# Loading 96 of 128 rows: two transfers of 48 rows in place of one of 128, from the fifth unit on

## The chip, the cores and the metric

The kernel runs on one core of one Trainium2 chip. The metric is device time in microseconds (us) of one execution, the median of several. A profiled execution gives a trace: each instruction with its engine, start and duration, what it waited for, and the packets that the 16 DMA engines moved. The engines are TensorE (PE, with its weight loads as PEld), VectorE (DVE), ScalarE (ACT), GpSimd (POOL) and SyncE (SP), which only issues transfers here.

## What is computed

A linear-attention layer whose state decays over time, and then a layer of eight experts of which each token uses one. Cut to what matters:

```python
def _attn_ref(r, k, v, w, u):                 # batch 4, heads 8, sequence 768, head size 48
    for t in range(S):
        cur = np.einsum('bhd,bhe->bhde', u[None] * kt, vt)
        y[:, :, t] = np.einsum('bhd,bhde->bhe', rt, state + cur)
        state = wt[:, :, :, None] * state + np.einsum('bhd,bhe->bhde', kt, vt)

def _moe_ref(x, ...):                         # 3072 tokens of 384 numbers, 8 experts, hidden size 1024
    e_idx = np.argmax(logits, axis=1)
    for e in range(E):
        h = np.maximum(x[mask] @ w1[e], 0.0)
        out[mask] = gate_w[mask, None] * (h @ w2[e])
```

## The kernel before

The attention part works through 24 units (`NU`), one for each batch element and stretch of 128 time steps. A unit holds all eight heads: heads come in pairs, and of the 128 partitions the first 48 rows belong to one head of each pair and rows 64 to 111 to the other. Rows 48 to 63 and 112 to 127 are padding: r and k are 0 and w is 1 there. The host lays r, k and w of a unit side by side in one array `rkw` of 128 rows by 1,541 numbers: r in columns 0 to 511, k in 512 to 1,023, w in 1,024 to 1,540.

Four buffers `ins[0..3]` (`NIN = 4`) of 128 partitions take turns: unit n is loaded into `ins[n % 4]`. `load(n, cuts)` of line 94 issues the transfers on SyncE's queue, one for each range of columns. Units 0 to 3 are loaded ahead of the loop. In the loop over i from -2 to 23, after the work of round i, SyncE issues in this order: v of unit i+3 (`loadv`, line 99), w of unit i+6, in some rounds a piece of a weight matrix (line 218, rounds 4 to 7 and from 18 on) or, later in the text, 128 rows of zeros to HBM (line 859, rounds 8 to 11), and r with k of unit i+6. A load into a buffer waits for those that read the buffer before: w for the scans of VectorE, r and k for GpSimd and ScalarE.

Round i (`att_iter`, line 287) works on three units at once. For unit a = i+2 VectorE runs a scan over w backward in time (line 295, giving B), takes four reciprocals, which it writes into w (297), and scans forward (298, giving E); GpSimd multiplies K from k and B (241) and G from r and k (306); ScalarE copies r into PSUM (235), and VectorE multiplies R (238). For unit m = i+1 TensorE transposes K (320) and multiplies K with R (345), VectorE masks the result (347), ScalarE copies v into zero-padded form (257), and TensorE adds to the state (359), which ScalarE scales (247). For unit z = i TensorE makes the output (372, 384, 387). VectorE or ScalarE with GpSimd forms the token rows (424, 421, 422), which TensorE transposes for the router (434, 440). In the rounds after the first ten units GpSimd also scatters the token rows to HBM, by expert (639). The order of the work is written out by hand; nothing is moved by a scheduler.

After some 120 us the expert blocks follow, bound by TensorE. Their first block reads rows that the scatters wrote. Later blocks read token rows in four loads of 32 partitions each (line 665).

Of the kernel before, what the change touches and what calls it, by code (L numbers as in the profile page):

```python
# [17 lines left out]
B, H, S, D = 4, 8, 768, 48  # L18
P = 128
# [39 lines left out]
def kernel(ctx: ExitStack, tc: tile.TileContext, rkw, vt, wf, cst, mid, wg, bias, w1, w2, out):  # L59
    nc = tc.nc  # L60
# [21 lines left out]
    NIN = 4  # L82
    ins = [pa.tile([P, 1600], F32, name=f"in{i}", bufs=1) for i in range(NIN)]
# [9 lines left out]

    def load(n, cuts=((0, 1541),)):
        for c0, c1 in cuts:
            nc.sync.dma_start(out=ins[n % NIN][:, c0:c1], in_=rkw[n, :, c0:c1])

    def loadv(n):
        nc.sync.dma_start(out=wt(n, "v", [P, VW], 4), in_=vt[n * P:(n + 1) * P, :])
# [4 lines left out]
    nc.vector.memset(wm, 0.0)  # L104
    cs = cp.tile([P, NCST], F32, name="cs")
    load(0, ((1024, 1541), (0, 1024)))
    load(1, ((1024, 1541),))
    nc.sync.dma_start(out=cs[:, 256:NCST], in_=cst[:, 256:NCST])
    loadv(0)
    load(1, ((0, 1024),))  # L110
    nc.gpsimd.memset(cs[:, 0:2 * P], 1.0)
    for c0, op in ((0, ALU.is_equal), (P, ALU.is_gt)):
# [1056 lines left out]
```

## Time and profile before

| what | value |
|---|---|
| median of 3 runs | 335.22 us (334.42 to 335.35) |
| the profiled execution | 336.19 us, of which the span of the trace 334.4 us |
| TensorE busy | 321.6 us, 96% of the span |
| TensorE weight loads | 293.1 us, 88% |
| VectorE busy | 214.4 us, 64% |
| ScalarE busy | 204.2 us, 61% |
| GpSimd busy | 196.6 us, 59% |
| moved by DMA | 58.66 MB, mean 175 GB/s |

TensorE's clock was granted at full speed almost throughout. Matmuls are pipelined and their ends are modelled, so a busy TensorE is not one at its peak. Shares over the whole span mix the attention rounds, where VectorE, GpSimd and ScalarE are nearly always busy, with the expert blocks, where they are not; a stage is to be read by itself. The chain that ended last, as the trace gives it, reaches back only 4 us from the end and says nothing of the attention rounds.

### The profile page before, as it was taken

To read this page: it belongs to the slowest core of one execution; us is meant where nothing else is said; L and a number is where in the kernel's file an instruction comes from. 1 tells how busy PE (TensorE), PEld (TensorE's weight loads), DVE (VectorE), ACT (ScalarE), POOL (GpSimd) and SP (SyncE) were. 2 spreads that over 40 slices of the span, in tenths; PEclk is the share of its full clock that TensorE was granted. 3 is DMA by queue.
4 is the path that set the end of the run, shared out by engine and by line. 5 is a ranking of instruction groups with operands and counts; after the bars stand their busy time and mean duration, and the time that the engine had idled before them with its cause. 6 is when DMAs were issued, how large, how long until landed. Compare 5 with 4: busy or idle time off the path is not lost. (4 is left out here: it accounts for less than half of the span.)

```text
span 334.4 us, 10126 instructions
## 1 busy us (share of the span) xinstructions
PE 321.6 (96%) x3942; PEld 293.1 (88%) x3943; DVE 214.4 (64%) x376; ACT 204.2 (61%) x467; POOL 196.6 (59%) x226
## 2 busy tenths in 40 slices
PE   6899998999999999999999999999999999999993
PEld 3689898988899988899889988998899889999993
DVE  6999997999999757795333965934560464054230
ACT  3887897787488775542521767656745855632150
POOL 7988987879999795676361680247024603450041
PEclk9999999999999999999999999999999999999998
DMA  7997888878998532426337037026544763360011
GB/s 273 406 347 245 294 280 241 285 243 240 301 309 263 163 97 97 95 95 215 143 119 213 0 84 250 0 73 169 185 167 165 214 233 97 95 212 5 0 74 32
DMA packets 35586, 58.66 MB, mean 175 GB/s; under 512 B 17297, under 2 KB 22089, under 8 KB 35528
## 3 DMA queue, kind: packets, MB, share of 16 engines
q1 hardware_dynamic: 32424, 48.45, 46.4%
q0 software_dynamic: 3104, 9.47, 7.6%
q8 instruction: 33, 0.54, 0.7%
q14 instruction: 25, 0.20, 0.2%
HBM read 57.86 MB, written 12.67 MB: 211 GB/s over the span
## 5 line engine op out<-in xcount | busy, mean ns | idle before, releaser
L224 POOL TENSOR_TENSOR wl<-raw,wh 128x768 fp32r<-128x768 f32 x20 | 39.0, 1954 | 73.8 <-ACT wh L223 73.7
L223 ACT CAST wh<-raw 128x768 fp32r<-128x768 f32 x48 | 39.3, 831 | 37.4 <-PE pU_d L731 23.3
L720 DVE SCALAR_TENSOR_TENSOR h<-pS_u,h 128x512 fp32r<-128x512 f32 (+2 forms) x39 | 23.2, 607 | 36.5 <-ACT h L718 36.3
L751 POOL DMA_INDIRECT out<-ot,xg x24 | 25.2, 1052 | 29.4 <-ACT ot L760 23.4
L224 DVE TENSOR_TENSOR wl<-raw,wh 128x768 fp32r<-128x768 f32 x28 | 31.0, 1113 | 14.8 <-ACT wh L223 14.4
L709 PE MATMUL pS_u<-xh,wh 128*128 128x512 f32 (+1 forms) x102 | 39.6, 388 | 0.0
L709 PE MATMUL pS_u<-xh,wl 128*128 128x512 f32 (+1 forms) x102 | 39.2, 385 | 0.0
L709 PE MATMUL pS_u<-xo,wh 128*128 128x512 f32 (+1 forms) x102 | 39.2, 384 | 0.0
L718 ACT ACTIVATE h<-pS_u 128x512 fp32r<-128x512 f32 (+1 forms) x34 | 19.8, 586 | 27.7 <-PE pS_u L709 25.4
L731 PE MATMUL pX_d<-wh,h 128*128 128x384 f32 x96 | 32.4, 337 | 0.0
L731 PE MATMUL pY_d<-wh,h 128*128 128x384 f32 x96 | 32.2, 335 | 0.0
L731 PE MATMUL pK_d<-wh,h 128*128 128x384 f32 x96 | 32.1, 334 | 0.0
L639 POOL DMA_INDIRECT xs<-xp,posT x24 | 26.1, 1088 | 9.3 <-issue 7.4
L306 POOL TENSOR_TENSOR G<-in 128x512 f32<-128x512 f32 x24 | 30.7, 1278 | 0.0
L241 POOL TENSOR_TENSOR K<-in,B 128x512 f32<-128x512 f32 x24 | 28.4, 1185 | 3.7 <-PE pY L387 1.7
L295 DVE TENSOR_TENSOR_SCAN B<-in,pX_d 128x516 f32<-128x516 f32 x24 | 29.3, 1219 | 1.8 <-DMA in<-rkw 1.8
L298 DVE TENSOR_TENSOR_SCAN E<-in,pX_d 128x516 f32<-128x516 f32 x24 | 29.5, 1229 | 0.8
L731 PE MATMUL pU_d<-wh,h 128*128 128x384 f32 x80 | 26.8, 334 | 0.0
L720 DVE SCALAR_TENSOR_TENSOR h<-pT_u,h 128x512 fp32r<-128x512 f32 (+2 forms) x17 | 9.6, 577 | 24.6 <-ACT h L718 24.6
L387 PE MATMUL pY<-v,A 128*64 128x48 f32 x368 | 25.3, 222 | 0.0
L347 DVE TENSOR_TENSOR A<-pS,m 128x768 f32<-128x768 f32 x24 | 22.8, 948 | 3.7 <-PE pS L345 3.6
L387 PEld LDWEIGHTS pY<-v,A 128*64 128x64 f32 x368 | 23.8, 138 | 0.0
(239 smaller groups left out, 860.8 us busy)
## 6 DMA issues: line engine op xcount, KB each, us to landing
raw<-w SPq DMA_DIRECT2D x24, 768.0 KB
in<-rkw SPq DMA_DIRECT2D x23, 512.0 KB
v<-vt SPq DMA_DIRECT2D x24, 288.0 KB
in<-rkw SPq DMA_DIRECT2D x23, 258.5 KB
wg<-wf SPq DMA_DIRECT2D x8, 576.0 KB
xl<-xs SPq DMA_DIRECT2D x20, 192.0 KB
raw<-w SPq DMA_DIRECT2D x16, 192.0 KB
xs<-zt SPq DMA_DIRECT2D x12, 193.0 KB
```

What stands on the lines that cost most here:

```text
L223: nc.scalar.copy(out=wh[k][:, sl], in_=raw[k][:, sl])
L224: (eng or (nc.vector, nc.gpsimd)[k]).tensor_tensor(out=wl[k][:, sl], in0=raw[k][:, sl], in1=wh[k][:, sl].bitcast(F32), op=ALU.subtract)
L241: nc.gpsimd.tensor_tensor(out=wt(a, "K", [P, 4, P]), in0=quarters(k), in1=quarters(T["B", a][:, 1:517])[:, :, 1:129], op=ALU.mult)
L295: nc.vector.tensor_tensor_scan(out=Bt[:, 516:0:-1], data0=w[:, 516:0:-1], data1=d1[:, 516:0:-1], initial=0.0, op0=ALU.mult, op1=ALU.max)
L298: nc.vector.tensor_tensor_scan(out=Et, data0=w[:, 0:516], data1=d1[:, 1:2].to_broadcast([P, 516]), initial=1.0, op0=ALU.mult, op1=ALU.max)
L306: nc.gpsimd.tensor_tensor(out=wt(a, "G", [P, 512]), in0=r, in1=k, op=ALU.mult)
L387: nc.tensor.matmul(out=yh[64:P, g, sw, hh], lhsT=A[:, hh, g, 1 + sw], rhs=vs[:, g, hh] if sw else v[:, h * D:(h + 1) * D], start=new and n ...
L639: rows_apart("xs", nc.gpsimd.indirect_dma_start(out=xs[:, :], out_offset=bass.IndirectOffsetOnAxis(ap=posT[:, n:n + 1], axis=0), in_=T["xp ...
L709: nc.tensor.matmul(out=pp, lhsT=wsrc[0][:, f, c * P:(c + 1) * P], rhs=xsrc[:, c], start=(n == 0), stop=(n == 3 * KC - 1))
L720: nc.vector.scalar_tensor_tensor(out=h2[:, o:o + c1 - c0], in0=pp[:, c0:c1], scalar=0.0, in1=hh[:, c0:c1].bitcast(F32), op0=ALU.max, op1=A ...
L731: nc.tensor.matmul(out=X["y", q][j], lhsT=hsrc[:, j * P:(j + 1) * P], rhs=wsrc[1][:, f], start=(f == 0 and n == 0), stop=(last and n == 2))
L751: ins = nc.gpsimd.indirect_dma_start(out=out[:, :], out_offset=bass.IndirectOffsetOnAxis(ap=xg[0:n, j, 1:2].bitcast(I32), axis=0), in_=ot[ ...
```

## The change

From the fifth unit on `load` issues, for each range of columns, two transfers in place of one: rows 0 to 47 and rows 64 to 111. The padding rows of a buffer are written by the first unit that it holds (units 0 to 3) and not again.

```diff
     def load(n, cuts=((0, 1541),)):
         for c0, c1 in cuts:
-            nc.sync.dma_start(out=ins[n % NIN][:, c0:c1], in_=rkw[n, :, c0:c1])
+            for q in (0, 64) if n >= NIN else (None,):
+                rows = slice(0, P) if q is None else slice(q, q + D)
+                nc.sync.dma_start(out=ins[n % NIN][rows, c0:c1], in_=rkw[n, rows, c0:c1])
```

`P` is 128 and `D` is 48. Each of units 4 to 23 is loaded with two ranges of columns, so its two transfers become four. All else is unchanged, the readers of the buffers included: they read all 128 rows.

## Rows read from the trace of the kernel before

**Rows 1.** Stretches of the span: us; busy time of PE, PEld, DVE, ACT, POOL; PEclk, DMA share, GB/s.

```profile
10.00:20.00 10.00, 8.70 (x208) 7.30 (x206) 9.86 (x13) 9.21 (x30) 9.70 (x18) 1.00 1.04 406
20.00:95.00 75.00, 72.00 (x1865) 66.28 (x1866) 70.87 (x102) 59.20 (x181) 65.50 (x72) 1.00 0.86 272
70.00:80.00 10.00, 9.50 (x251) 8.77 (x250) 9.83 (x15) 7.83 (x25) 8.88 (x9) 1.00 0.66 201
80.00:90.00 10.00, 8.98 (x235) 8.25 (x233) 9.67 (x14) 6.91 (x22) 9.60 (x10) 1.00 0.95 294
90.00:100.00 10.00, 9.99 (x263) 9.29 (x259) 9.62 (x14) 7.00 (x22) 9.44 (x10) 1.00 0.93 304
```

**Rows 2.** VectorE in order of time: start us, us, what, and idle time before it.

```profile
46.38 1.22 DVE L295 TENSOR_TENSOR_SCAN B<-in,pX_d 128x516 f32<-128x516 f32 x1
51.03 1.22 DVE L295 TENSOR_TENSOR_SCAN B<-in,pX_d 128x516 f32<-128x516 f32 x1
55.51 0.96 DVE L347 TENSOR_TENSOR A<-pS,m 128x768 f32<-128x768 f32 x1 [1.78 <-PE pS L345]
56.98 1.22 DVE L295 TENSOR_TENSOR_SCAN B<-in,pX_d 128x516 f32<-128x516 f32 x1
80.76 1.22 DVE L295 TENSOR_TENSOR_SCAN B<-in,pX_d 128x516 f32<-128x516 f32 x1
85.29 1.22 DVE L295 TENSOR_TENSOR_SCAN B<-in,pX_d 128x516 f32<-128x516 f32 x1
88.63 0.96 DVE L347 TENSOR_TENSOR A<-pS,m 128x768 f32<-128x768 f32 x1 [0.19 <-PE pS L345]
90.10 1.22 DVE L295 TENSOR_TENSOR_SCAN B<-in,pX_d 128x516 f32<-128x516 f32 x1
```

**Rows 3.** Waits of the compute engines: us in total, times, longest us.

```profile
DVE B L295 <- DMA in<-rkw: 1.8, 1, 1.8
POOL K L241 <- DMA in<-rkw: 1.2, 2, 0.7
```

**Rows 4.** Order of time, SyncE's issues and the readers of what they load.

```profile
44.77 0.33 SPq L96 DMA_DIRECT2D in<-rkw  x1
47.77 0.33 SPq L99 DMA_DIRECT2D v<-vt  x1
59.74 0.71 ACT L257 COPY vz<-v 64x192 f32<-64x192 f32 x2
61.20 1.22 DVE L295 TENSOR_TENSOR_SCAN B<-in,pX_d 128x516 f32<-128x516 f32 x1
```

**Rows 5.** TensorE in order of time, and the instruction queue from 20 to 95 us.

```profile
53.25 0.24 PE L384 MATMUL pY<-vz,A 128*64 128x96 f32 x1 [1.10 <-issue]
84.33 0.57 PE L272 MATMUL pT<-cs,G 128*64 128x2 f32 x13 [1.02 <-issue]
q8 instruction: 14, 0.23, 1.2%
```

**Rows 6.** Four loads of 32 rows: their issue, and the stretch (columns as rows 1).

```profile
134.46 1.97 SPq L665 DMA_DIRECT2D xl<-xs  x4
135.40:139.40 4.00, 4.00 (x32) 3.21 (x31) 3.67 (x9) 2.72 (x6) 2.85 (x3) 1.00 1.00 198
```

**Rows 7.** Lines 96 and 295: duration ns min/median/max, first and last start.

```profile
L96 SPq DMA_DIRECT2D in<-rkw x47: 327/328/506, 0.8 to 94.8; - x47
L295 DVEq EVENT_SEMAPHORE  x22: 21/21/21, 3.6 to 106.9; - x22
```

**Rows 8.** Waits of SyncE's queue: us in total, times, longest us.

```profile
SPq L96 <- DVE E L298: 18.3, 16, 2.2
SPq L99 <- PE pY L387: 16.4, 13, 2.6
SPq L96 <- DMA in<-rkw: 1.9, 4, 0.8
```

**Rows 9.** The page's queue of SyncE's transfers: packets, MB, share of 16 engines.

```profile
q1 hardware_dynamic: 32424, 48.45, 46.4%
```

## The prediction

> **What bounds the kernel now.** I read the busy time by stage first, then VectorE's order of time, the waits, SyncE's order of time, and TensorE's idle stretches. The change lies in the attention rounds, up to 95 us, where the last load of r, k and w is issued [rows 7]. In the 75 us from 20 to 95, VectorE is busy 70.87 us and TensorE 72.00; the share of the 16 DMA engines is 0.86 at 272 GB/s [rows 1]. So the attention rounds run at the pace of VectorE and TensorE, with the DMA engines nearly full beside them. A round is one start of the backward scan of line 295 to the next: 4.53 us from 80.76 to 85.29, 4.65 from 46.38 to 51.03 [rows 2]. What follows the rounds depends on them, so a microsecond lost in them is taken as one lost at the end.
>
> Does any engine wait for r, k and w? VectorE did once, 1.8 us, before its first scan, and GpSimd twice, 1.2 us in total, at the first units [rows 3]. After that none does. The reason is the lead: the w load issued at 44.77 goes into the buffer that the scan of unit 9 has just left, and is read four scans later, at 61.20, so 16.4 us on; the v load issued at 47.77 is read at 59.74, 12.0 us on [rows 4]. Fewer bytes thus buy nothing directly. What can move is what shares the DMA engines with them.
>
> That something is seen in two places. TensorE stands idle 1.10 us before 53.25 and 1.02 us before 84.33, each in the middle of a run of equal matmuls and with "issue" as the reason: it waited for nothing that the trace names [rows 5]. From 20 to 95 us queue 8 brought 14 packets of instructions, 0.23 MB, so 16 KB each [rows 5]; TensorE ran 1,865 matmuls and 1,866 weight loads in that time [rows 1], 266 for each packet or some 62 B per instruction, while VectorE ran 102. I read queue 8 as TensorE's instruction refills, one a round, and the two idle stretches as refills that came late because they share the DMA engines with the loads. They cost: VectorE's operation of line 347 waited 1.78 us for TensorE and that round lasted 5.95 us in place of 4.65; at the second it waited 0.19 and the round lasted 4.81 in place of 4.53 [rows 2]. Of 2.12 us of idle TensorE 1.58 passed on, a factor of 0.75. In the stretch with the DMA share at 0.66 there is no late refill; at 0.95 there is one, at 0.93 none [rows 1].
>
> **The change, part by part.** Bytes: a unit's r, k and w are 128 rows of 1,541 numbers, 788,992 B; they become 96 rows, 591,744 B, for 20 of 24 units, so 3.94 MB less.
>
> DMA time per byte: from 70 to 80 us, where almost only these loads and v run, a share of 0.66 moved 201 GB/s [rows 1], so 305 GB/s while busy, and one unit's r, k, w take 2.59 us of all 16 engines. Afterwards: if a byte costs the same, 1.94 us, 0.65 less. No load of 48 rows stands in the trace. The nearest are four loads of 32 rows each, issued from 134.46: from 135.4 to 139.4 the share was 1.00 and the rate 198 GB/s [rows 6]. At that rate a unit takes 2.99 us, 0.40 more than before with a quarter fewer bytes. These four also come in pieces of 384 B where the rows here are 2,068 and 4,096 B, so part of their slowness may be the pieces'. I take 2.99, the only row with few partitions, and keep 1.94 for the range. The DMA engines' work in a round is now 0.86 of 4.53 us, 3.9 us; it becomes 4.30 us, a share of 0.95, or at the other end 3.25 us, 0.72.
>
> The Trainium skill has a rule against this change (SBUF — State Buffer, "Door 1: The DMA port swizzle" and "Can I just issue two DMAs to hit both halves?"): partitions 0 to 63 reach only half of the ports through which DMA enters SBUF, 196 GB/s against 328 for a 1 MiB load, and two loads on the two halves together gained 6% over one. An estimate from that page's 196 GB/s is 3.0 us per unit, and the sum would be the same as mine; the row with 198 GB/s agrees with it, and no row shows 48 rows.
>
> Refills: those between 20 and 95 us, 14 of them, now wait behind 0.40 us more per round. At the least the two late ones come 0.40 us later each and nothing else changes: 0.8 times 0.75, 0.6 us. At the most every second refill is late, by 1.06 us as the two are now and 0.40 more: 7 times 1.46 less the present 2.12 is 8.1, times 0.75, 6.1 us. No row is nearer to either end; I take the middle, **3.3 us**.
>
> SyncE: 40 more issues at a median of 0.328 us, 13.1 us in all [rows 7]. Covered: its queue waits 18.3 us for VectorE's second scan and 16.4 us for TensorE before v loads [rows 8]. In a round it would issue two more, 0.66 us; behind them stand v, the weight pieces and the zero rows, whose nearest reader is 12.0 us away. Its queue also waits 1.9 us in four places for the landing of an earlier transfer [rows 8]; with five transfers a round for three this can only grow, under the same cover. Taken at nothing; without the cover 0.66 us a round.
>
> Waits: the scan of line 295, K, G and the copy of r now need two landings. Before 22 of the 24 scans stands one wait of 21 ns of its own on VectorE's sequencer [rows 7]; one more for 20 units is between nothing and 0.42 us. I take nothing, since such waits stand on the sequencer and not among the busy operations; on GpSimd and ScalarE, busy 65.50 and 59.20 of 75 us [rows 1], a wait as short is covered. The padding rows keep r and k of 0 and w of 1 from the first four units; the reciprocal that writes into w puts 1 there again.
>
> The start: from 10 to 20 us the DMA engines run at 1.04 and 406 GB/s [rows 1], with the fifth to seventh unit among the transfers. The work that waits there is behind by what the halves cost, ahead by the quarter that is gone; taken at nothing, between a gain and a loss of 0.5 us (one unit's 0.40 to 0.65 us).
>
> Sum: +3.3 us. The profiled execution took 336.19 us with a span of 334.4; it stands 0.97 us above the median. So 339.5 us for such an execution, and 335.22 + 3.3 = **338.5 us** for the median.
>
> **The rivals.** *Fewer bytes, lighter queue.* If the halves run at the old rate, the share falls to 0.72, near the 0.66 of the stretch without late refills. Both vanish: 2.12 times 0.75, 1.6 us less, **333.6 us**. For it: the pieces of 384 B may be why the 32-row loads are slow. Against it: that stretch is the only evidence with few partitions. It decides from 305 GB/s down to about 228, at which 96 rows cost as much as 128.
>
> *Nothing that can be measured.* The halves overlap so far that a unit takes 2.6 us as before (some 228 GB/s), and refills fall as they do now: **335.2 us**, within 1 us. That is also the case in which the change does not do what it says: fewer bytes, but no less time on the DMA engines.
>
> *The loads become the bound.* A round has room for 4.53 less the 1.31 us of other transfers, 3.22 us, so from 184 GB/s down the loads fall behind, and 198 is not far above. At half the old rate, 152 GB/s, a unit takes 3.89 us, 0.67 too long, 13.4 us over 20 units; the lead of 12.0 us less one round's transfers of 3.9 takes 8.1 of it, 5.3 remain, and with the refills' upper end of 6.1 the time is **346.6 us**. Then scans would wait for the loads. By the same page's table 48 rows leave eight rows on each of four ports, as many as 128 rows did; two halves one after the other would take twice 2.59 us, and the sum would lie above this rival.
>
> **How the numbers follow.** Forecast 0.38, with its own range of 335.8 to 341.3 (its ends 0.6 and 6.1 us); loads as bound 0.12; no difference 0.23; faster 0.27. So slower by over 0.3% (1.0 us, about what a measurement of this kernel can tell from no change) 0.50, within it 0.23, faster 0.27. The range from 333.0 to 344.5 reaches below the faster rival and leaves out most of the case with the loads as bound and the start's gain on top of the faster one.
>
> **What would show it.** Queue 1: 3.94 MB less than 48.45, and fewer rows but 40 more transfers [rows 9]. The DMA share from 20 to 95 us: about 0.95 if I am right, 0.72 for the faster rival. TensorE: more than two idle stretches before "issue", of 1 us and over, and rounds of 5 us and more; none in the faster case. VectorE waiting for in after 20 us: the loads as bound. The prediction is wrong if the share falls while bytes fall with it, or if refills do not follow the share.

## The result, and the profile after

| | before | after |
|---|---|---|
| median of the runs made beside each other | 335.29 us | 338.89 us |
| lowest to highest | 333.96 to 339.57 | 336.15 to 340.94 |
| the profiled execution, and its span | 336.19, 334.4 | 340.48, 338.7 |

The ratio is 1.0095, with an interval of 1.0074 to 1.0116: slower by 3.2 us. Ratios leave out executions more than 1.5% above the fastest of their kernel. The forecast was 338.5 us.

The stretches of the kernel after, with the columns of [rows 1]. Its lines from 96 on stand 2 higher than those of before (295 is 297, 347 is 349).

```profile
10.00:20.00 10.00, 7.07 (x170) 5.73 (x170) 9.86 (x14) 8.91 (x27) 9.94 (x19) 1.00 0.98 285
20.00:95.00 75.00, 72.52 (x1867) 66.82 (x1864) 69.31 (x99) 59.26 (x181) 64.18 (x71) 1.00 0.90 232
12.00:18.00 6.00, 5.21 (x134) 4.48 (x133) 5.86 (x8) 5.51 (x17) 5.94 (x16) 1.00 0.98 255
20.00:60.00 40.00, 38.08 (x977) 35.04 (x974) 35.18 (x49) 32.83 (x102) 33.08 (x37) 1.00 0.99 237
60.00:95.00 35.00, 34.44 (x897) 31.78 (x893) 34.13 (x51) 26.43 (x80) 31.10 (x35) 1.00 0.81 228
```

The last three stretches in the kernel before:

```profile
12.00:18.00 6.00, 5.21 (x154) 4.71 (x155) 5.86 (x9) 5.62 (x17) 5.71 (x11) 1.00 1.03 407
20.00:60.00 40.00, 38.54 (x999) 35.30 (x1000) 36.84 (x52) 33.81 (x103) 34.03 (x38) 1.00 0.87 275
60.00:95.00 35.00, 33.47 (x872) 30.99 (x870) 34.03 (x51) 25.39 (x79) 31.47 (x35) 1.00 0.84 268
```

Fewer bytes, and no less work for the DMA engines. From 12 to 18 us they were full, as before (shares of 0.98 and 1.03), and moved 255 GB/s in place of 407. From 20 to 60 us the share rose from 0.87 to 0.99; only from 60 us on did it fall, from 0.84 to 0.81. From 20 to 95 us that is 0.90 for 0.86 in [rows 1].

The page's queue of SyncE's transfers (packets, MB, share of 16 engines) says the same for the whole span: against [rows 9], 3.94 MB less and a share of 46.9 in place of 46.4%.

```profile
q1 hardware_dynamic: 31784, 44.51, 46.9%
```

TensorE in order of time, all stretches of 0.25 us and over from 12 to 112 us in which it stood idle and nothing that the trace names was awaited (the idle time stands in brackets):

```profile
19.10 0.45 PE L274 MATMUL pT<-cs,G 128*64 128x2 f32 x10 [1.43 <-issue]
39.07 0.55 PE L374 MATMUL pY<-SPb,R 128*64 128x96 f32 x8 [0.77 <-issue]
50.66 0.20 PE L389 MATMUL pY<-v,A 128*64 128x48 f32 x1 [0.92 <-issue]
95.77 0.24 PE L361 MATMUL pU_st<-v,KT 128*48 128x48 f32 x1 [0.30 <-issue]
106.18 0.46 PE L374 MATMUL pY<-SPb,R 128*64 128x96 f32 x5 [0.65 <-issue]
```

Before there were two, those of [rows 5], together 2.12 us; now there are five, together 4.07 us, and three of them come before 51 us. VectorE passes them on: its operation of line 349 waited for the matmuls of line 347. The three starts of the backward scan below (units 10, 11 and 12) answer to the first, second and fourth of [rows 2].

```profile
42.36 0.96 DVE L349 TENSOR_TENSOR A<-pS,m 128x768 f32<-128x768 f32 x1 [0.63 <-PE pS L347]
47.34 0.96 DVE L349 TENSOR_TENSOR A<-pS,m 128x768 f32<-128x768 f32 x1 [0.82 <-PE pS L347]
48.82 1.22 DVE L297 TENSOR_TENSOR_SCAN B<-in,pX_d 128x516 f32<-128x516 f32 x1
53.09 0.96 DVE L349 TENSOR_TENSOR A<-pS,m 128x768 f32<-128x768 f32 x1 [1.58 <-PE pS L347]
54.56 1.22 DVE L297 TENSOR_TENSOR_SCAN B<-in,pX_d 128x516 f32<-128x516 f32 x1
59.41 1.22 DVE L297 TENSOR_TENSOR_SCAN B<-in,pX_d 128x516 f32<-128x516 f32 x1
```

The round with the wait of 1.58 us lasted 5.74 us, from 48.82 to 54.56; in the kernel before the same round lasted 4.65 [rows 2]. After 10.1 us no operation of a compute engine waited for r, k or w. Until then VectorE, ScalarE and GpSimd had waited for units 0 and 1, which the change loads as before. GpSimd's issue of the scatters waited once later, 0.9 us. The starts of the backward scan show where the time went, in us by which a unit's scan starts later than in the kernel before (from VectorE's order of time in each trace; the last two columns are the first matmul of the first expert block and the span):

```
unit             1     4     5     8     9    10    11    12    15    19    23  block   span
before        7.13 19.31 24.12 37.51 42.04 46.38 51.03 56.98 71.72 90.10 108.53 121.35 334.4
after        +0.45 +0.47 +1.06 +1.07 +1.79 +2.44 +3.53 +2.43 +2.42 +2.14  +2.33  +4.48  +4.3
```

The steps at units 5, 9 and 11 stand behind the idle stretches that end at 19.10, 39.07 and 50.66. Behind the step of 0.65 at unit 10 the trace shows only one of 0.23 us, which ends at 44.79. The step down at unit 12 is the round in which the kernel before has its own, at 53.25 [rows 5]. From unit 12 to the last scan no more is lost than in the kernel before. The 0.45 us of the start is there at unit 1, whose load the change leaves alone, so it is this execution's. At the first expert block another 2.15 us came on top, which later runs of the same loads don't show (below). There TensorE waited 1.89 us for the block's token rows, in place of 0.36 us; before, then after:

```profile
121.35 0.72 PE L687 MATMUL pX_x<-cs,xl 128*128 128x128 f32 x4 [0.36 <-DMA xl<-xs]
125.83 0.73 PE L689 MATMUL pX_x<-cs,xl 128*128 128x128 f32 x4 [1.89 <-DMA xl<-xs]
```

### The profile page after: what moved, and what is told of

Its sections match the earlier page's. It is cut to its first block, busy times and chain, and to the rows that moved or that the text cites. A ratio compares the mean times of both kernels' runs of the same rounds, so it can differ in the third digit from the quotient of the medians.

```text
span 338.7 us, 10201 instructions
## 1 busy us (share of the span) xinstructions
PE 323.1 (95%) x3943; PEld 293.7 (87%) x3943; DVE 214.8 (63%) x376; ACT 204.1 (60%) x467; POOL 196.8 (58%) x226
## 3 DMA queue, kind: packets, MB, share of 16 engines
q1 hardware_dynamic: 31784, 44.51, 46.9%
```

## The experiments

The edits are to `load`, in the kernel before, unless said. A diff is cut to the lines that matter; where it shows added lines alone, they stand in place of the one transfer in `load`, except for the added load, which stands behind it. The theory: transfers of fewer than 128 rows take the DMA engines longer per byte, the share stays high, and TensorE's instruction refills behind them come late. The rivals: it is the number of transfers; it is the late refills alone, whatever the rate; it is waits at the added landings.

**Halves with all bytes.** The split without the saving of bytes: two transfers of 64 rows.

```diff
-            nc.sync.dma_start(out=ins[n % NIN][:, c0:c1], in_=rkw[n, :, c0:c1])
+            for q in (0, 64) if n >= NIN else (None,):
+                rows = slice(0, P) if q is None else slice(q, q + 64)
+                nc.sync.dma_start(out=ins[n % NIN][rows, c0:c1], in_=rkw[n, rows, c0:c1])
```

> From the fifth unit on two transfers of 64 rows each, so all 128 rows, padding included, in halves. Theory of the halves (a load that reaches half of the partitions takes more DMA time per byte): if the rate in GB/s is what stays, a third more bytes than with 48 rows, DMA share from 20 to 95 us at 0.97 or more, 6 us or more slower than before. If instead the fullest ports set the time (eight rows on each of them with 48 rows as with 64), the same as the changed kernel, 2 to 5 us slower than before. Rival, the number of transfers: the same as the changed kernel, about 3 us slower, but with packets of 4,096 B as fast as before. Rival, halves cost nothing: within 1 us of before.

Measured: 349.4 us, 1.0386 [1.0324, 1.0448]. From 12 to 18 us 297 GB/s at a share of 1.05, no operation of a compute engine waiting for r, k and w after 12 us (GpSimd's issue of the scatters did, 1.4 us), and eight idle stretches of TensorE before "issue", 9.2 us.

```profile
12.00:18.00 6.00, 4.55 (x130) 4.04 (x130) 5.86 (x9) 5.62 (x17) 5.73 (x11) 1.00 1.05 297
20.00:95.00 75.00, 69.23 (x1699) 63.79 (x1695) 62.87 (x90) 55.55 (x170) 57.08 (x64) 0.94 0.96 248
```

**Twice the transfers at 128 rows.** Each range of columns in two, so four transfers a unit, as many as after the change, with all rows and all bytes.

```diff
+            mid = (c0 + c1) // 2
+            for d0, d1 in ((c0, mid), (mid, c1)) if n >= NIN else ((c0, c1),):
+                nc.sync.dma_start(out=ins[n % NIN][:, d0:d1], in_=rkw[n, :, d0:d1])
```

> From the fifth unit on as many transfers as the changed kernel (four a unit), but each of 128 rows and half of the columns; all bytes are loaded. Theory of the halves: within 1 us of before, 10 to 20 us at some 400 GB/s. Rival, the number of transfers (issues on SyncE, transfers held until an earlier one has landed, waits for two landings): 2 to 4 us slower than before, as the changed kernel.

Measured: 337.04 us, 1.0034 [0.9999, 1.0069].

```profile
12.00:18.00 6.00, 5.33 (x158) 4.82 (x158) 5.86 (x9) 5.52 (x16) 5.56 (x11) 1.00 1.05 388
```

The rate stays (388 GB/s), and in the trace the last scan starts 0.2 us later than before. So the number of transfers, SyncE's added issues and the added landings cost some 1.1 us by the ratio, and 2.3 us at the upper end of its interval: less than the change, though perhaps not nothing.

**The bytes of the change at 128 rows.** One transfer of all rows and three quarters of the columns.

```diff
+            d1 = c1 if n < NIN else {1024: 768, 1541: 1412}[c1]
+            nc.sync.dma_start(out=ins[n % NIN][:, c0:d1], in_=rkw[n, :, c0:d1])
```

> From the fifth unit on one transfer of 128 rows for each range of columns, but only three quarters of the columns of r with k and of w, so the bytes of the changed kernel; the rest of a buffer keeps the columns of an earlier unit, so that part of r, k and w is not the unit's own. Theory: DMA share from 20 to 95 us at 0.70 to 0.78, no late refill or short ones, 1 to 2 us faster than before. Rival, fewer bytes are worth nothing because the loads are hidden and refills do not depend on them: within 0.7 us of before.

Its whole time, 404.58 us, can't be compared: with other numbers in r, k and w the tokens go to the experts differently, and TensorE runs 4,110 matmuls in place of 3,942. Its attention rounds can:

```profile
12.00:18.00 6.00, 5.22 (x155) 4.72 (x156) 5.86 (x9) 5.57 (x16) 5.50 (x11) 1.00 1.02 396
20.00:95.00 75.00, 73.52 (x1907) 67.92 (x1909) 72.32 (x104) 60.77 (x186) 66.82 (x73) 1.00 0.78 230
```

396 GB/s, a share of 0.78, one idle stretch of 0.49 us, and the last scan 1.9 us earlier than before (106.59 for 108.53). In the rounds a quarter fewer bytes is worth something if it is saved in full-height transfers.

**More DMA work and nothing else.** One load more per unit, of 240 columns (123 KB), into a tile that nothing reads.

```diff
+        if n >= NIN and cuts[0][0] == 0:
+            nc.sync.dma_start(out=dummy, in_=rkw[n, :, 0:240])
```

> The kernel before with one more load a unit from the fifth unit on, of 128 rows and 240 columns (122,880 B, some 0.40 us of the DMA engines) into a tile that nobody reads. Theory that DMA time as such makes the refills late: share from 20 to 95 us at 0.93 to 0.97, four or more idle stretches of TensorE before issue, 1.5 to 4 us slower than before. Rival, it is something of the halves alone (two landings to wait for, their order): within 1 us of before.

Measured: 341.37 us, 1.0185 [1.0128, 1.0241], 6 us.

```profile
20.00:95.00 75.00, 71.38 (x1763) 65.76 (x1762) 66.73 (x96) 56.42 (x172) 63.59 (x69) 0.95 0.92 298
58.71 0.26 PE L390 MATMUL pY<-v,A 128*64 128x48 f32 x2 [1.08 <-issue]
87.09 0.57 PE L275 MATMUL pT<-cs,G 128*64 128x2 f32 x13 [1.37 <-issue]
```

More DMA work alone makes this kernel slower, with no reader of the added bytes, but hardly by more stops: four or more had been expected, and there are two, of 2.45 us in place of 2.12. What differs is TensorE's clock behind them. It fell behind both stops, while behind the two of the kernel before it stayed at 1.00:

```profile
57.00:65.00 8.00, 6.92 (x128) 6.50 (x125) 6.12 (x8) 3.46 (x10) 6.47 (x7) 0.79 0.89 263
84.00:92.00 8.00, 6.63 (x130) 6.05 (x128) 6.45 (x10) 3.86 (x12) 7.76 (x8) 0.79 0.97 303
```

The scans fell behind at these two places: against the kernel before, unit 12 started 0.6 us early, unit 15 2.2 us late and unit 19 4.4 us late. So this run doesn't show that fuller DMA engines make more refills late. ScalarE also waited 0.8 us for v.

**One transfer of 112 rows.** If what makes the halves slow is that each reaches only one half of the partitions, a transfer of rows 0 to 111 should run as 128 rows do.

```diff
+            rows = slice(0, P) if n < NIN else slice(0, 64 + D)
+            nc.sync.dma_start(out=ins[n % NIN][rows, c0:c1], in_=rkw[n, rows, c0:c1])
```

> From the fifth unit on one transfer of 112 rows (0 to 111) for each range of columns in place of one of 128: an eighth fewer bytes, no more transfers, both halves of the partitions in one transfer. Theory of the halves: bytes as fast as with 128 rows, DMA share from 20 to 95 us at 0.80 to 0.86, packets of the loads undisturbed, 0 to 1 us faster than before. Rival, any load of fewer than 128 rows is slow per byte: 1 to 3 us slower than before.

Measured: 342.08 us, 1.0178 [1.0138, 1.0217].

```profile
12.00:18.00 6.00, 4.60 (x131) 4.10 (x130) 5.86 (x9) 5.62 (x17) 5.68 (x11) 1.00 1.04 282
18.73 0.46 PE L273 MATMUL pT<-cs,G 128*64 128x2 f32 x10 [1.53 <-issue]
32.65 0.34 PE L360 MATMUL pU_st<-v,KT 128*48 128x48 f32 x7 [2.27 <-issue]
```

282 GB/s at a share of 1.04: as slow per byte as two halves, with one transfer over both. The halves are not the cause.

**Where the cost arises.** The changed kernel, with the split for units 14 to 23 only, and for units 4 to 13 only.

```diff
-            for q in (0, 64) if n >= NIN else (None,):
+            for q in (0, 64) if n >= 14 else (None,):          # late
+            for q in (0, 64) if NIN <= n < 14 else (None,):    # early
```

> The changed kernel's halves from unit 14 on only; units 4 to 13 in one transfer of 128 rows as before. Theory: the trace after lost its time in the rounds up to unit 11, where weight pieces and zero rows share the DMA engines, and nothing later; so within 1 us of before, and it may be faster. Rival, each unit in halves costs the same: 10 of 20 units, 1.6 us slower than before.

> The halves for units 4 to 13 only; from unit 14 on one transfer of 128 rows. Theory: the whole loss of the changed kernel or more, 2.5 to 4.5 us slower than before. Rival, each unit costs the same: 1.6 us slower.

Measured: late 335.6 us, 1.001 [0.9983, 1.0037]; early 339.72 us, 1.0152 [1.0117, 1.0187]. The cost comes from the first ten units with the split, and the later ten cost nothing that can be measured. The early split alone costs 5.1 us by the ratio, more than all twenty units did (3.2); why is open. Late, then early:

```profile
20.00:60.00 40.00, 39.59 (x1036) 36.47 (x1036) 38.13 (x54) 34.43 (x105) 35.39 (x39) 1.00 0.87 269
60.00:95.00 35.00, 33.98 (x866) 31.50 (x862) 34.16 (x51) 25.89 (x79) 31.49 (x35) 1.00 0.82 232
```

```profile
20.00:60.00 40.00, 36.67 (x949) 33.78 (x946) 33.77 (x48) 31.85 (x99) 31.64 (x36) 1.00 0.93 232
60.00:95.00 35.00, 33.56 (x859) 30.97 (x858) 34.12 (x51) 25.60 (x79) 30.77 (x34) 1.00 0.84 263
```

**Three transfers, all bytes.** Rows 0 to 31, 32 to 95 and 96 to 127, so that one transfer spans the middle.

```diff
+            for q0, q1 in ((0, 32), (32, 96), (96, P)) if n >= NIN else ((0, P),):
+                nc.sync.dma_start(out=ins[n % NIN][q0:q1, c0:c1], in_=rkw[n, q0:q1, c0:c1])
```

> From the fifth unit on three transfers for each range of columns, rows 0 to 31, 32 to 95 and 96 to 127: all bytes, six transfers a unit. The middle one has 64 rows like the halves of 64, but half of them on either side of partition 64. Theory that it matters which partitions a transfer reaches: less DMA time than with the two halves of 64 (13.0 us slower than before), 2 to 8 us slower than before. Rival, the number of transfers or their rows: as slow as the halves of 64 or slower, 13 us and more.

Measured: 352.04 us, 1.048 [1.0458, 1.0502], and 264 GB/s at 0.93 from 12 to 18 us. It was expected that a transfer over the middle would make this cheaper than the 64-row halves, and it is dearer. But the run can't separate the two theories, since here SyncE's queue is the bound: six issues a round took over 4 us of it, at a DMA share of 0.82 from 20 to 95 us, and v, issued behind them, came late. First such a row of issues, then waits of the compute engines from 12 to 122 us (us in total, times, longest us):

```profile
61.33 4.28 SPq L97 DMA_DIRECT2D in<-rkw  x6
ACT vz L258 <- DMA v<-vt: 8.1, 6, 1.9
PE pU_st L360 <- DMA v<-vt: 4.9, 4, 1.7
```

**Moving other transfers away.** If the share in the early rounds decides, moving other early transfers should help: the weight pieces eight rounds later, the zero rows four rounds earlier; once in the kernel before, once in the changed one.

```diff
-            if i == (n + 4 if n < FC // 2 else NU - 10 + n if n < FC else NU - 6 + (n - FC) // 2):
+            if i == (n + 12 if n < FC // 2 else NU - 10 + n if n < FC else NU - 6 + (n - FC) // 2):
-        if 8 <= i < 8 + JT:
+        if 4 <= i < 4 + JT:
```

> The kernel before, loads of 128 rows, with other DMA work moved out of the busiest rounds: the four pieces of the first weight matrix from rounds 4 to 7 to rounds 12 to 15, the four zero transfers from rounds 8 to 11 to rounds 4 to 7. Nothing is left out. Theory that a DMA queue that is too full makes the instruction refills late: DMA share from 20 to 60 us at 0.75 to 0.82 in place of 0.87, the idle stretch before 53 us gone, 0.8 to 1.8 us faster than before. Rival, the idle stretches have another cause: the stretch stays and the time is within 0.5 us of before.

> The changed kernel with the same move of weight pieces and zero transfers. Theory: the halves have less beside them in rounds 4 to 11, so fewer late refills, 1 to 2.5 us faster than the changed kernel, 0.5 to 2.5 us slower than before; the idle stretch near 19 us, ahead of round 4, stays. Rival, the halves cost something else than refills: 3 us slower than before, as the changed kernel.

Measured: on before 337.12 us, 1.0038 [1.0008, 1.0068]; on the changed kernel 338.88 us, 1.0072 [1.0041, 1.0104]. Neither helped: the first is slower by 1.3 us, the second can't be told from the change itself. On before the share from 20 to 60 us stayed at 0.87 and the idle stretch near 53 stayed where it was, 0.92 us. On the changed kernel the share did fall, from 0.99 to 0.86, yet three stops of 1.2 to 1.3 us are left, together 3.84 us in place of 4.07, and the granted clock fell behind each:

```profile
20.00:60.00 40.00, 38.70 (x950) 35.99 (x946) 33.84 (x48) 31.88 (x99) 30.96 (x35) 0.94 0.86 219
```

So this move is no remedy, and a lower share over a stage does not by itself bring the refills in time.

**Are they refills?** The changed kernel with `NWARM` 15 in place of 12: three more warm-up matmuls ahead of the loop and one more in it. With its weight load each, TensorE's program has eight instructions more before 12 us, and nothing else differs.

> The changed kernel with 4 more pairs of weight load and matmul (8 instructions) on TensorE at the start, in time in which it waits for data anyway: three in the first warm-up and one in the second. Theory that the idle stretches are instruction refills, at fixed counts of TensorE's instructions: the stretch near 19 us stands 8 instructions earlier in the program, before a run of 14 matmuls of line 274 (14 of 16 left) in place of 10; the others move likewise by 4 matmuls. Rival, they belong to what the instruction does or waits for: they stand where they stood, before a run of 10.

A single execution, 339.19 us. Five of its six stops, TensorE in order of time:

```profile
18.30 0.57 PE L274 MATMUL pT<-cs,G 128*64 128x2 f32 x14 [1.28 <-issue]
38.40 0.72 PE L374 MATMUL pY<-SPb,R 128*64 128x96 f32 x12 [0.95 <-issue]
45.08 0.24 PE L386 MATMUL pY<-vz,A 128*64 128x96 f32 x1 [1.14 <-issue]
51.50 0.20 PE L389 MATMUL pY<-v,A 128*64 128x48 f32 x1 [1.44 <-issue]
97.12 0.33 PE L361 MATMUL pU_st<-v,KT 128*48 128x48 f32 x5 [0.27 <-issue]
```

Compare the first two and the last with the changed kernel: behind the stop there were 10, 8 and 1 matmuls of the run to go, here 14, 12 and 5. The stops moved four matmuls, eight instructions with their weight loads, back in the program: just what was put in ahead. A stop that hangs on data or on a semaphore would have stayed at its instruction. So the stops sit at fixed counts of instructions, as refills must. (Without added instructions the same stops stand at 10 or 11 and at 7 or 8 in the other kernels, so a shift of four is clear of that scatter.)

The trace's records of single DMA packets say it a second way. Each stop of the kernels before and after ended 1.3 to 1.7 us after a 16 KB packet of queue 8 had ended, though such packets come 3.5 to 6.7 us apart:

```
             packet of queue 8    TensorE stood idle   packet's end to restart, us
before       50.84 to  51.76       52.15 to  53.25         1.49
             82.02 to  83.00       83.31 to  84.33         1.33
after        16.30 to  17.68       17.67 to  19.10         1.42
             36.18 to  37.34       38.30 to  39.07         1.73
             47.70 to  49.06       49.74 to  50.66         1.60
             93.00 to  94.30       95.47 to  95.77         1.47
            102.94 to 104.81      105.53 to 106.18         1.37
```

Over the thirteen profiled executions that holds for all 48 stops of 0.25 us and over between 12 and 112 us, with 1.2 to 1.8 us. So a stop is the wait for such a packet. In the 3 us ahead of these 48 packets the DMA share was 0.86 to 1.06, in the mean 1.01; ahead of the other 190 it was 0.88 in the mean, and at 0.95 or over for 72 of them. A late refill follows a full stretch, but not every full stretch makes one late.

**The runs side by side.** Idle time of TensorE before "issue" from 12 to 112 us (stretches of 0.25 us and over) beside the start of the last backward scan, for the profiled executions in which the granted clock was 1.00 from 20 to 95 us:

```
                                idle us   last scan against before, us
bytes of the change, 128 rows     0.49      -1.9
split from unit 14 on             1.05      -1.5
before                            2.12       0
before, other transfers moved     2.94      +0.4
after                             4.07      +2.3
after, eight instructions more    5.67      +3.2
split for units 4 to 13           6.15      +3.3
```

From the first line to the last 5.66 us of idle TensorE go with 5.2 us, 0.9 of it. As far as these seven executions show, the change's loss in the rounds is these stops. In the last two lines, and in the kernel with the late split, the first expert block starts as late against before as the last scan did, within 0.5 us (+2.9, +2.8 and -1.2). So the 2.15 us that the profiled execution of after lost there as well did not come again with the same loads. Most of it is the longer wait for the block's token rows; why these came later is open.

## Why the prediction was right

**Direction and size.** Forecast +3.3 us; measured 3.2 by the ratio, 3.6 by the medians. **The mechanism** held in outline: no operation waits for r, k and w after the start; the DMA engines are no emptier with a quarter of these bytes gone; refills come late; VectorE passes that on. That the size came out to a tenth of a microsecond is luck, as the terms below show.

**Bytes.** 3.94 MB, to the second digit.

**DMA time of a unit: right in sign, off in both levels.** The prediction took 2.59 us before and 2.99 after, from 305 and 198 GB/s [rows 1, 6]. Where the engines are full, from 12 to 18 us, they moved 407 / 1.03 = 395 GB/s before and 255 / 0.98 = 260 after (other transfers included), which makes 2.00 us and 2.28 us: +0.28 for +0.40. (Three other traces of the same loads give 259 to 272 GB/s there.) The step that failed is the choice of rows: a stretch with a share of 0.66 for the old rate, when [rows 1] had a full one at 406; and the 32-row loads, whose 198 GB/s is lower than any transfer of 48 to 112 rows gave (255 to 297). That the rate differs between a full stretch and a half-full one was not weighed; from 60 to 95 us it was 268 / 0.84 = 319 before and 228 / 0.81 = 281 after, and there the share fell a little.

**The share.** 0.95 foretold from 20 to 95 us, 0.90 found, as 0.99 and then 0.81. The prediction spread the cost evenly over the rounds. It lies in the first half alone, as the kernels with the split early and late show. That the weight pieces and zero rows of those rounds are the reason is not shown, since moving them away did not help. The prediction called itself wrong if refills did not follow the share. Over the stage from 20 to 95 us they don't: the 112-row kernel had a share of 0.87 and 5.17 us of stops, the changed kernel with other transfers moved 0.86 and 3.84, while the kernel with the added load had 0.92 and 2.45 and the one with twice the transfers at 128 rows 0.89 and 1.62. Only in the 3 us ahead of a refill do late ones and full engines go together. That link of the argument was too coarse.

**Late refills.** "Every second of 14, by 1.46 us" was the upper end, with a factor of 0.75; the middle of the bounds was taken. Found: five stops of 4.07 us in place of two of 2.12, so 1.95 us more, passed on at about 0.9. That is 1.8 us in this execution, and 3.2 in the run with eight instructions more, which has the same loads. The sum came out by a middle between wide bounds and not by knowing which refills fall late; a single execution scatters by as much. Nor do the stops lie where the sum put them. From 20 to 95 us, whose 14 refills it counted, this execution has 1.69 us of stops in place of 2.12; the longest, 1.43 us, ends at 19.10, in the start, which the sum took at nothing and which cost some 0.6 us at unit 5. (The run with eight instructions more has 4.12 us from 20 to 95.) The refills' packets there took 1.02 us in the mean before and 1.29 after, 0.27 more, of the 0.40 that the sum added; what a packet waited before its start the trace doesn't show. Only one stop was over 1 us, where "more than two" had been foretold; the three rounds of over 5 us before unit 12 (5.40, 5.25 and 5.74) agree.

**The clock, a term that the sum lacked.** The mean granted clock of after's 22 executions was 0.992; that of 56 executions of before, made beside the experiments, 0.996. Among those 56 a clock lower by 0.01 goes with 3.0 us more, among the 22 with 1.8. An estimate from these: 0.7 to 1.2 us of the 3.2 go with the clock and not with the stops themselves. In after's profiled execution the clock stayed at 1.00 in the rounds, so its trace doesn't show this part.

**SyncE and the added landings at nothing.** Near enough: twice the transfers at full height cost about 1.1 us, with an interval from 0 to 2.3. But its queue's waits for landings of in and v grew from 3.6 us (1.9 of them in [rows 8]) to 13.5, and those for VectorE and TensorE shrank by as much or more:

```profile
SPq L98 <- DVE E L300: 6.7, 10, 1.2
SPq L98 <- DMA in<-rkw: 6.5, 10, 2.5
SPq L101 <- PE pY L389: 4.6, 5, 1.9
SPq L98 <- DMA v<-vt: 3.7, 6, 1.3
```

(with 2.2 and 1.1 us more for in and v ahead of v loads). The cover of 12 us that the prediction named held in the changed kernel. With six transfers a unit it did not, and v came late. The prediction's list of waits leaves out ScalarE's for r at units 0 and 1, 3.1 and 0.5 us, and one of 1.0 us of GpSimd at 24.28; no term rests on them.

**The rivals.** The faster one had its mechanism right and its condition wrong: at the old rate the rounds gain 1.9 us (1.6 had been worked out), but halves don't run at the old rate. For "no difference" 228 GB/s had been worked out as the rate at which 96 rows cost as much as 128; by the full stretches that point is 0.75 times 395, 296 GB/s, and the halves were below it. A wait for loads came in only with three transfers per range, and there it was v, behind SyncE's issues.

**The rule of the Trainium skill.** The Trainium skill (SBUF — State Buffer, "Door 1: The DMA port swizzle" and "Can I just issue two DMAs to hit both halves?") led to the same sum, for a reason that the runs don't bear out. Its 196 GB/s for half of the ports, measured on a 1 MiB load, is below the 255 GB/s measured here (other transfers included); and by its table of ports rows 0 to 111 reach all of them, but one transfer of these rows ran at 282 GB/s, as slow as halves. What it concludes there, that only one transfer spanning all 128 partitions hits all 16 ports, agrees in its advice with every run, since only such transfers were fast. What beneath makes fewer rows slow is open: the trace doesn't show how the rows are dealt out to the DMA engines.

## What to carry to other kernels

Bytes that nobody waits for are not worth saving by lowering the height of a transfer: look first at what the DMA engines are full of, and cut columns rather than rows if it can be done (in the rounds here that gained 1.9 us, where cutting rows lost 2.3). Where DMA is near full beside a long TensorE program, count TensorE's idle stretches before "issue" in every trace, since they tell the cost of the next load before any engine waits for data, and read the granted clock behind each, since a stop can cost more by the clock than by its own length. A price should come from a row with the same share of the resource as the stretch that decides.

## What the runs showed of the hardware

**The height of a transfer.** In the kernels without an added load the transfers of 128 rows moved 388 to 407 GB/s from 12 to 18 us, in whatever pieces (half the columns, three quarters, all); all of 32 to 112 rows, one or two or three together, 255 to 297, at shares of 0.93 to 1.05. The packets themselves got longer: from 14 to 20 us one of 4,096 B took 160 ns in the mean in the kernel before, 283 with 48-row halves, 255 with 64-row halves and 258 in the transfers of 112 rows.

**A late instruction refill.** TensorE's program comes over the same DMA engines in packets of 16 KB. One that comes late stops TensorE in the middle of a run of matmuls, here for 0.3 to 2.3 us, and the restart follows the packet's end by 1.2 to 1.8 us, in 48 of 48 stops.

**A stop can cost the clock.** In the kernel with 64-row halves TensorE stood idle 1.56 us at 17 us, and from 18 to 24 us the granted clock was 0.51, which is the lower of its two levels, 1.2 GHz; four equal transposes took 1.12 us there and 0.66 later. The changed kernel stood idle 1.43 us at the same place, and the early split 1.72, and both kept 1.00. Of the 26 stops of 0.9 us and over from 12 to 112 us in all thirteen traces, 11 were followed by 4 us at a mean clock under 0.8. Their length doesn't tell which: the shortest of these was 0.90 us, and the longest that kept 1.00 was 2.19 us. What decides is open.

```profile
18.70 0.80 PE L274 MATMUL pT<-cs,G 128*64 128x2 f32 x11 [1.56 <-issue]
18.00:24.00 6.00, 5.29 (x71) 5.21 (x72) 4.44 (x6) 2.08 (x8) 5.10 (x5) 0.51 0.93 226
23.14 1.12 PE L322 MATMUL pK<-cs,K 128*128 128x128 f32 x4
28.59 0.66 PE L322 MATMUL pK<-cs,K 128*128 128x128 f32 x4
```

The kernels that lost more than their stops are those with a lower clock: the 64-row halves started the last scan 10.6 us late with 9.2 us of stops against 2.1, and 112 rows 6.9 us late with 5.2, at a mean clock of 0.94 and 0.93 from 20 to 95 us.
